# Moving sixteen blocks of transposes and a reused key/value group in a two-layer attention kernel: where the kept group is scored, and where its values are turned

## The chip, the cores and the metric

The kernel runs on one core of one Trainium2 chip. Times are device microseconds (us) of whole executions. The profile is one execution taken by the hardware profiler, so its span is one sample. All timed runs used here are undisturbed (fast).

## The reference

Two layers, each attention with cached keys and values followed by an MLP, run forward and then backward from `grad_out`. Both layers use the same caches and the same weights.

```python
x = A_x                                   # [2, 1, 1024]
x = x + attn(layernorm(x), k_cache, v_cache, wq, wo)   # layer 0
x = x + mlp(layernorm(x), w1, b1, w2, b2)              # the mlp has a layernorm of its own
x = x + attn(layernorm(x), k_cache, v_cache, wq, wo)   # layer 1
x = x + mlp(layernorm(x), w1, b1, w2, b2)
# outputs: x and the gradients of x, both caches, wq, wo, w1, b1, w2, b2
# caches: [2, 4, 16384, 128] bf16, 33.5 MB each; 32 query heads, 8 for each key/value head
```

Batch and key/value head together make `G` = 8 *groups*. A group's keys are four *chunks* of 1 MB, and so are its values. A layer's attention reads 67 MB of cache, and the caches are read by both layers, forward and backward.

## The kernel before

Loads go through a ring of seven 1 MB buffers (pool `ld`) and are all issued by one queue, in program order. A load is issued when the buffer of the seventh load before it is released. The last group (`G - 1` = 7) is *kept*: layer 0 loads its eight chunks into tiles of their own, and later uses load nothing. One more chunk, the first of group `XG` = 3, is kept in the same way (tiles `keepxK` and `keepxV`).

```python
    NLD = 7                                # load buffers of 1 MB
    ld = ctx.enter_context(tc.tile_pool(name="ld", bufs=NLD))
    # ...
    def turn(view, new_tp):                # transposes eight 128x128 blocks in place
        tp = new_tp()
        for o in range(8):
            PE.transpose(tp[:, o, :], view[:, o * 128:(o + 1) * 128], ident[:])
        evac_bf16(view, tp[:].rearrange("p a b -> p (a b)"), 1024)   # ScalarE or VectorE
    # ...
    def kv_load(w, g, c):
        keep = w + str(c) if g == G - 1 else w if (g, c) == (XG, 0) else None
        t = held_tiles[keep] if keep else ld.tile([128, LDW], BF16, name="kv_" + w, tag="ld")
        if keep not in held:
            src = Kv if w == "K" else Vv
            nc.sync.dma_start(t[:]..., src[g, :, c * TC:(c + 1) * TC, :])
            if keep:
                held.add(keep)
        return t[:].rearrange("p (t d) -> p t d", d=128)
```

The attention forward walks through slots, four to a chunk. A slot transposes 1024 keys (8 transposes) and scores those of two slots ago (8 matmuls). When a group's 16 slots are over, its softmax and its products with V follow, spread over the slots of the next group, beginning nine slots later.

```python
    def attn_fwd(l, q_bf, rbc, oT, groups):
        sch = Sched()
        slots = [(g, c, b) for g in groups for c in range(NCH) for b in range(NB)]
        # ... post(g): row maximum, 16 exponentials, sch.later(9, quads of chunks 0, 1),
        #     sch.later(13, quads of chunks 2, 3), evacuation, finish
            def finish(ps):
                V.tensor_tensor(out=oT[:, g, :], in0=ps, in1=rbc[:, g, :], op=ALU.mult)
        # ...
        while s < len(slots) + 2 or sch.busy():
            # ... emit_T(cv, b, True); sch.run_slot(...); score(s - 2)
    # ...
        attn_fwd(l, qT_bf, rbc, oT, ALLG)          # groups 0..7, the kept one last
```

The backward attention of layer 1 transposes V instead, and needs the kept group's V transposed. That is done there by the 16 *turns* (`v_turns`), one in every third slot. The kept group's own slots, which load and transpose nothing, lie between the slots of the third and the fourth group.

```python
    def attn_bwd(l, do_bf, dqT, dn, groups, ahead):     # groups 0, 4, 3, 1, 5, 2, 6
        slots = []
        for i, g in enumerate(groups):
            for c in range(NCH):
                for b in range(NB):
                    slots.append((g, c, b))
                    if 2 <= i < 2 + NCH // 2 and c % 2 == 0:
                        slots.append((G - 1, (i - 2) * 2 + c // 2, b))
        # ...
        v_turns = deque(lambda c=c, b=b: turn(held_tiles["V%d" % c][:, b * 1024:(b + 1) * 1024], ...)
                        for c in range(NCH) for b in range(NB))
        while s < len(slots) + 2 or sch.busy():
            # ...
                    kTs[s] = emit_T(cv, b, True)
                    if s % 3 == 2 and s >= 8 and v_turns:
                        v_turns.popleft()()
            # ...
            if dots and s % 3 < 2:          # dot products on VectorE with wq tiles of the ring
                dots.popleft()()
```

Of the kernel before, what the change touches and what calls it, by code (L numbers as in the profile page):

```python
# [9 lines left out]
BF16 = mybir.dt.bfloat16  # L10
# [13 lines left out]
def kernel(  # L24
# [25 lines left out]
    V = nc.vector  # L50
# [13 lines left out]
    G = B * HKV  # L64
    T = SK // 128
    TC = 32
    NCH = T // TC
# [254 lines left out]
    def turn(view, new_tp):  # L322
# [4 lines that stand above are left out]
        evac_bf16(view, tp[:].rearrange("p a b -> p (a b)"), 1024)  # L327
# [176 lines left out]

    def attn_fwd(l, q_bf, rbc, oT, groups):
        sch = Sched()
        slots = [(g, c, b) for g in groups for c in range(NCH) for b in range(NB)]
        kTs, sc, st = {}, {}, {}

        def max_half(g, f):  # L510
            m = small.tile([128, 8], F32, name="mx%d" % f)
            V.tensor_reduce(out=m[:], in_=sc[g][f][:], axis=AX.X, op=ALU.max)
            charge("D", 0.7)
            st[g].append(m)

        def post(g):
            max_half(g, 1)
            m0, m1 = st[g]
            V.tensor_tensor(out=m0[:], in0=m0[:], in1=m1[:], op=ALU.max)
            esum = small.tile([128, 2, 8], F32, name="esum")  # L520
            negm = small.tile([128, 8], F32, name="negm")
            box = {}

            def p1():
                box["pm"] = pm_([8, 128], F32, "pm")
                PE.transpose(box["pm"][:, :], m0[:], identf[:])
                gm = small.tile([8, 1], F32, name="gm")
                V.reduce_max(out=gm[:], in_=box["pm"][:, :], axis=AX.X)
                box["dg"] = small.tile([8, 8], F32, name="dg")
                V.tensor_scalar(out=box["dg"][:], in0=identf[0:8, 0:8], scalar1=gm[:, 0:1], scalar2=None, op0=ALU.mult)  # L530
                charge("D", 0.5)

            def p2():
                pm2 = pm_([128, 8], F32, "pm2")
                PE.matmul(pm2[:], lhsT=onesf[0:8, :], rhs=box["dg"][:], start=True, stop=True)
                V.tensor_scalar(out=negm[:], in0=pm2[:], scalar1=-1.0, scalar2=None, op0=ALU.mult)  # L536
                charge("D", 0.2)

            def ex(f, h):
                half = NP // 2  # L540
                S.activation(out=e_all[:, g, f * half:(f + 1) * half, l, h, :],  # L541
                             in_=sc[g][f][:, h, :].rearrange("p (a b) -> p a b", b=2),
                             func=ACT.Exp, bias=negm[:, h:h + 1], scale=1.0, accum_out=esum[:, f, h:h + 1])
                charge("A", 0.3)

            def fin1():
                V.tensor_tensor(out=esum[:, 0, :], in0=esum[:, 0, :], in1=esum[:, 1, :], op=ALU.add)

            def fin2():
                pm3 = part_sum(esum[:, 0, :], 8, "pm3")  # L550
                V.reciprocal(out=rbc[:, g, :], in_=pm3[:])

            def finish(ps):
                V.tensor_tensor(out=oT[:, g, :], in0=ps, in1=rbc[:, g, :], op=ALU.mult)

            a = Acc(g, "V", lambda u: e_all[:, g, u, l].rearrange("p h t -> p (h t)"), finish, g % 2)
            sch.later(2, p1)
            sch.later(4, p2)
            for i in range(16):
                sch.later(5 + i // 2, lambda i=i: ex(i // 8, i % 8))  # L560
            sch.later(9, lambda: queue_acc(sch, a, range(0, 2), False))
            sch.later(13, lambda: queue_acc(sch, a, range(2, 4), True))
            sch.later(14, fin1)
            sch.later(15, fin2)

        def score(s):
            g, c, b = slots[s]
            if c == 0 and b == 0:
                sc[g] = {}
                st[g] = []  # L570
            kT = kTs.pop(s)
            for j in range(8):
                t = c * TC + b * 8 + j
                f = t // TH
                if t % TH == 0:
                    sc[g][f] = px([128, 8, TH], F32, "sc")
                PE.matmul(sc[g][f][:, :, t % TH], lhsT=kT[:, j, :], rhs=q_bf[:, g, :], start=True, stop=True)  # L577
            if c == NCH // 2 - 1 and b == NB - 1:
                max_half(g, 0)
            if c == NCH - 1 and b == NB - 1:  # L580
                post(g)

        cv = None
        s = 0
        while s < len(slots) + 2 or sch.busy():
            sch.s = s
            if s < len(slots):
                g, c, b = slots[s]
                if b == 0:
                    cv = kv_load("K", g, c)  # L590
                kTs[s] = emit_T(cv, b, True)
            sch.run_slot(1 if s < len(slots) else 2)
            if 2 <= s < len(slots) + 2:
                score(s - 2)
            s += 1

    def attn_bwd(l, do_bf, dqT, dn, groups, ahead):
        sch = Sched()
        wq_q, wq_n, w2_q = deque(), {}, deque()
        slots = []  # L600
        for i, g in enumerate(groups):
            for c in range(NCH):
                for b in range(NB):
                    slots.append((g, c, b))
                    if 2 <= i < 2 + NCH // 2 and c % 2 == 0:
                        slots.append((G - 1, (i - 2) * 2 + c // 2, b))
        kTs, sc, accs = {}, {}, {}
        made = {"n": 0}
        done_g = []
# [60 lines left out]
        def score(s):  # L670
# [7 lines left out]
            if b == NB - 1:  # L678
# [1 line left out]

        cv = None
        s = 0
        v_turns = deque(lambda c=c, b=b: turn(held_tiles["V%d" % c][:, b * 1024:(b + 1) * 1024],
                                              lambda: pt([128, 8, 128], BF16, "turn"))
                        for c in range(NCH) for b in range(NB))
        while s < len(slots) + 2 or sch.busy():
            sch.s = s
            if s < len(slots):
                g, c, b = slots[s]
                if g == G - 1:  # L690
                    kTs[s] = kept_vT(c)[:, b * 8:(b + 1) * 8, :]
                else:
                    if b == 0:
                        cv = kv_load("V", g, c)
                    kTs[s] = emit_T(cv, b, True)
                    if s % 3 == 2 and s >= 8 and v_turns:
                        v_turns.popleft()()
                if g == groups[-1] and b == 1 and c == 0:
                    n = wq_n[g % HKV] = wq_steps(l, g % HKV, dqT, dn, lambda: pt([128, 8, 128], BF16, "wtq"),
                                                 lambda: px([128, 512], F32, "dn_ps"))  # L700
                    for k, f in enumerate(n[0]):
                        wq_q.append(lambda f=f, k=k, n=n: (f(), n[2][4 * k]()))
                        wq_q.extend(n[2][4 * k + 1:4 * k + 4])
            sch.run_slot(1 if s < len(slots) else 2)
            if 2 <= s < len(slots) + 2:
                score(s - 2)
            if wq_q and (s % 2 == 1 or len(wq_q) > 6):
                wq_q.popleft()()
            if dots and s % 3 < 2:
                dots.popleft()()  # L710
            s += 1
# [39 lines left out]
    def attn_layer_fwd(l, xT):  # L751
        y, rstd = ln_fwd(xT[:], f"a{l}")
        V.tensor_copy(out=n_all[:, :, lsl(l)], in_=y[:])
        qps, _ = w_pass(A_wq, D, HD, "q_ps", xT_bf=n_all[:, :, lsl(l)])
        qT_bf = vec.tile([128, G, 8], BF16, name=f"qT_bf{l}")
        for b in range(2):
            V.tensor_scalar(out=qT_bf[:, b * HKV:(b + 1) * HKV, :].rearrange("p k r -> p (k r)"), in0=qps[:, :, b],
                            scalar1=QSCALE, scalar2=None, op0=ALU.mult)
        rbc = vec.tile([128, G, 8], F32, name=f"rbc{l}")
        oT = vec.tile([128, G, 8], F32, name=f"oT{l}")  # L760
        attn_fwd(l, qT_bf, rbc, oT, ALLG)
        for b in range(2):
            V.tensor_copy(out=o_all[:, :, 2 * l + b], in_=oT[:, b * HKV:(b + 1) * HKV, :].rearrange("p k r -> p (k r)"))
        aps, _ = w_pass(A_wo, HD, D, "a_ps", xT_bf=o_all[:, :, lsl(l)])
        xn = vec.tile([128, DJ, 2], F32, name=f"xA{l}")
        V.tensor_tensor(out=xn[:], in0=aps[:], in1=xT[:], op=ALU.add)
        saved[f"a{l}"] = dict(y=y, rstd=rstd, qT_bf=qT_bf, rbc=rbc, oT=oT)
        return xn
# [695 lines left out]
```

## Time and profile before

| | |
|---|---|
| median of 3 runs | 1150.4 us (1148.43 to 1152.41) |
| bytes moved | 449.3 MB, mean 391 GB/s |
| highest rate that a stretch holds | about 424 GB/s |

The first lines are of the page of the kernel before. The GB/s line has 40 slices of 28.8 us each.

```profile
span 1150.5 us, 39958 instructions
...
GB/s 371 423 425 424 425 424 412 407 353 357 423 424 424 423 318 423 394 355 406 376 420 421 340 366 357 318 281 304 374 405 423 419 421 421 424 422 420 424 422 248
```

At 424 GB/s the 449.3 MB take 1060 us, so the transfers bound the kernel and the rest is hollows in this line. The unit of this document is the *lost time* of a stretch: its length times (1 - GB/s / 424). The sum of lost time is what a schedule can win or lose, since both kernels move the same bytes.

The next fence is the windows view of the kernel before. Each row gives a stretch (us), its length, the busy time of TensorE (PE), its weight loads, VectorE, ScalarE and GpSimd with the number of instructions, then the granted TensorE clock, the busy share of the DMA engines, and GB/s. The rows are the first 50 us after the layer-1 query projection (the *head*), the end of that attention forward with the output projection (the *tail*), and the first 60 us, the middle and the last 50 us of the backward attention.

```profile
272.50:322.50 50.00, 44.86 (x951) 40.00 (x952) 26.18 (x55) 24.23 (x90) 0.00 (x0) 0.94 1.01 424
400.00:440.00 40.00, 28.50 (x592) 22.25 (x590) 12.80 (x44) 10.94 (x67) 1.38 (x2) 0.69 0.89 346
502.50:562.50 60.00, 57.34 (x1258) 48.27 (x1259) 32.94 (x73) 26.96 (x47) 0.00 (x0) 1.00 0.95 367
562.50:617.50 55.00, 48.26 (x958) 39.56 (x956) 31.98 (x76) 27.10 (x49) 0.00 (x0) 0.91 1.01 422
617.50:667.50 50.00, 37.99 (x749) 31.21 (x747) 22.37 (x64) 21.58 (x39) 0.00 (x0) 0.86 0.97 372
```

Lost time: head 0, tail 40 x (1 - 346/424) = 7.4 us, backward 8.1 us in the first 60 us, 0.3 in the middle and 6.1 at the end. In the first 60 us TensorE is busy 57 of 60.

The tile view of the kernel before says where the turns are and what one costs (minimum/median/maximum ns, then first and last start):

```profile
L326 PE MATMUL turn<-ident,keepV x128: 217/219/219, 509.5 to 563.3; 128*128 128x128 bf16 x128
L161 DVE COPY keepV<-turn x8: 690/691/692, 510.1 to 544.4; 128x1024 bf16<-128x1024 bf16 x8
L158 ACT COPY keepV<-turn x8: 586/587/593, 513.5 to 563.6; 128x512 int32<-128x512 int32 x8
```

The load queue at the head, from its timeline (start, time taken, line, what is loaded). Seven K tiles are issued as the query weights leave the ring. Then each release brings the next load: in these lines every 2.6 to 3.2 us, from 4 us after the projection on, and the transfers never run dry:

```profile
265.15 7.48 SPq L413 DMA_DIRECT2D kv_K<-in_A_k_cache_dram  x7
276.83 0.33 SPq L413 DMA_DIRECT2D kv_V<-in_A_v_cache_dram  x1
280.05 0.33 SPq L413 DMA_DIRECT2D kv_K<-in_A_k_cache_dram  x1
282.63 0.33 SPq L413 DMA_DIRECT2D kv_V<-in_A_v_cache_dram  x1
285.22 0.33 SPq L413 DMA_DIRECT2D kv_K<-in_A_k_cache_dram  x1
```

Three pieces of the same stretch, TensorE's timeline of the kernel before: a slot of transposes and scores repeats every 0.65 us.

```profile
281.35 0.61 PE L424 MATMUL tp<-ident,kv_K 128*128 128x128 bf16 x8
281.80 0.35 PE L577 MATMUL sc<-qT_bf,kT 128*128 128x8 bf16 x8
282.00 0.61 PE L424 MATMUL tp<-ident,kv_K 128*128 128x128 bf16 x8
```

### The profile page before, as it was taken

How to read it: one execution, taken by the hardware profiler on the slowest of the kernel's cores; microseconds unless marked ns; L12 is line 12 of the kernel's file. 1: busy time of each engine (PE TensorE's matmuls, PEld its weight loads, DVE VectorE, ACT ScalarE, POOL GpSimd, SP SyncE). 2: the span in 40 equal slices, each digit the busy share in tenths (PEclk: the TensorE clock that was granted, in tenths of full speed). 3: DMA queues.
4: the chain of work that ended last, by engine and by line, in shares of the span. 5: the costliest groups of instructions: out<-in, count | busy, mean ns of one | idle time of the engine just before them, and what ended most of it. 6: DMA issues, size and time to landing. Idle time of an engine off the chain costs nothing. (4 is left out here: it accounts for less than half of the span.)

```text
span 1150.5 us, 39958 instructions
## 1 busy us (share of the span) xinstructions
PE 956.2 (83%) x17581; PEld 732.7 (64%) x17581; DVE 632.4 (55%) x1335; ACT 567.0 (49%) x1417; POOL 63.9 (6%) x113
## 2 busy tenths in 40 slices
PE   4989795487879876899987799788898999998885
PEld 3867674487767755888776698665555554554452
DVE  1535451133545433454845365667777867787684
ACT  0544351022535430344454455567676867786673
POOL 0000000000000000000000000001111112111111
PEclk9988895587999975899997899797777967898785
DMA  9999999998999989999999999877999999999996
GB/s 371 423 425 424 425 424 412 407 353 357 423 424 424 423 318 423 394 355 406 376 420 421 340 366 357 318 281 304 374 405 423 419 421 421 424 422 420 424 422 248
DMA packets 89130, 449.30 MB, mean 391 GB/s; under 512 B 7026, under 2 KB 7026, under 8 KB 49788
## 3 DMA queue, kind: packets, MB, share of 16 engines
q1 hardware_dynamic: 72204, 348.17, 75.0%
q0 software_dynamic: 16752, 98.59, 20.7%
q8 instruction: 137, 2.24, 0.7%
q14 instruction: 37, 0.30, 0.1%
HBM read 348.14 MB, written 98.58 MB: 388 GB/s over the span
## 5 line engine op out<-in xcount | busy, mean ns | idle before, releaser
L158 ACT COPY kT<-tp 128x512 int32<-128x512 int32 x209 | 122.8, 587 | 252.5 <-PE tp L424 243.6
L161 DVE COPY kT<-tp 128x1024 bf16<-128x1024 bf16 x159 | 108.6, 690 | 110.8 <-PE tp L424 97.6
L424 PE MATMUL tp<-ident,kv_K 128*128 128x128 bf16 x1728 | 144.6, 233 | 4.3 <-DMA kv_K<-in_A_k_cache_dram 4.3
L424 PEld LDWEIGHTS <-kv_K 128*128 128x128 bf16 x1728 | 109.7, 104 | 5.0 <-DMA kv_K<-in_A_k_cache_dram 4.9
L169 DVE CAST big<-xm 128x512 bf16<-128x512 f32 x142 | 92.3, 685 | 31.8 <-PE xm L1242 13.9
L166 ACT CAST big<-xm 128x512 bf16<-128x512 f32 x155 | 84.4, 593 | 25.9 <-PE xm L1144 15.5
L577 PEld LDWEIGHTS <-kT 128*128 128x128 bf16 x2048 | 76.3, 98 | 27.0 <-issue 22.0
L577 PE MATMUL sc<-qT_bf,kT 128*128 128x8 bf16 x2048 | 91.8, 171 | 0.0
L274 PE MATMUL wtp<-ident,wt 128*128 128x128 bf16 x928 | 77.8, 233 | 3.7 <-issue 2.3
L424 PE MATMUL tp<-ident,kv_V 128*128 128x128 bf16 x864 | 70.9, 229 | 10.3 <-DMA kv_V<-in_A_v_cache_dram 8.8
L541 ACT ACTIVATE e_all<-sc,negm 128x64 bf16<-128x64 f32 x256 | 77.1, 343 | 1.1 <-DVE negm L536 1.0
L310 PEld LDWEIGHTS <-wt 128*128 128x128 bf16 x1696 | 48.8, 103 | 43.6 <-issue 14.7
L169 DVE CAST keepK<-xm 128x512 bf16<-128x512 f32 x95 | 61.6, 684 | 16.2 <-PE xm L1242 9.6
L456 PE MATMUL acc_all<-kv_V,e_all 128*16 128x256 bf16 x864 | 46.2, 294 | 27.9 <-DMA kv_V<-in_A_v_cache_dram 13.8
L161 DVE COPY wT<-wtp 128x1024 bf16<-128x1024 bf16 (+1 forms) x64 | 40.5, 636 | 49.0 <-PE wtp L274 45.9
L158 ACT COPY wT<-wtp 128x512 int32<-128x512 int32 (+1 forms) x60 | 34.5, 576 | 65.5 <-PE wtp L274 56.8
L166 ACT CAST keepK<-xm 128x512 bf16<-128x512 f32 x102 | 54.8, 592 | 24.1 <-PE xm L1242 21.3
L166 ACT CAST keepV<-xm 128x512 bf16<-128x512 f32 (+1 forms) x98 | 53.1, 594 | 22.5 <-PE xm L1242 18.9
L424 PEld LDWEIGHTS <-kv_V 128*128 128x128 bf16 x864 | 55.9, 102 | 11.9 <-DMA kv_V<-in_A_v_cache_dram 9.5
L274 PEld LDWEIGHTS <-wt 128*128 128x128 bf16 x928 | 59.6, 104 | 4.4 <-issue 3.1
L541 ACT ACTIVATION_READ_ACCUMULATOR e_all<-sc,negm 128x1 f32 x256 | 59.8, 234 | 0.0
L169 DVE CAST keepV<-xm 128x512 bf16<-128x512 f32 (+1 forms) x74 | 48.0, 684 | 15.3 <-PE xm L1242 12.7
(352 smaller groups left out, 1775.8 us busy)
## 6 DMA issues: line engine op xcount, KB each, us to landing
kv_K<-in_A_k_cache_dram SPq DMA_DIRECT2D x81, 1024.0 KB, 12.2
kv_V<-in_A_v_cache_dram SPq DMA_DIRECT2D x81, 1024.0 KB, 12.1
out_dram<-big POOLq DMA_DIRECT2D x36, 1024.0 KB, 17.4
wt<-in_A_wo_dram SPq DMA_DIRECT2D x32, 1024.0 KB, 10.0
wt<-in_B_w_dram SPq DMA_DIRECT2D x32, 896.0 KB, 14.0
out_dram<-keepK POOLq DMA_DIRECT2D x22, 1024.0 KB, 17.3
out_dram<-keepV POOLq DMA_DIRECT2D x18, 1024.0 KB, 17.1
wt<-in_A_wq_dram SPq DMA_DIRECT2D x16, 1024.0 KB, 8.8
```

The lines of the kernel that those rows point to most:

```text
L158: S.copy(out=dst.bitcast(I32), in_=src.bitcast(I32))
L161: V.tensor_copy(out=dst, in_=src)
L166: S.copy(out=dst, in_=src)
L169: V.tensor_copy(out=dst, in_=src)
L274: PE.transpose(tp[:, o, :], wv[:, j, (o0 + o) * 128:(o0 + o + 1) * 128], ident[:])
L310: PE.matmul(fps[:, jo, :].rearrange("p (a b) -> p a b", b=2), lhsT=wv[:, j, jo * 128:(jo + 1) * 128], rhs=xT_bf[:, j0 + j, :].unsqueeze(1) ...
L424: PE.transpose(tp[:, j, :], cv[:, b * 8 + j, :], ident[:])
L456: PE.matmul(self.acc[cg:cg + 16, :], lhsT=coef(u), rhs=self.cv[:, t:t + 2, :].rearrange("p t d -> p (t d)"), start=False, stop=True, tile_ ...
L541: S.activation(out=e_all[:, g, f * half:(f + 1) * half, l, h, :], in_=sc[g][f][:, h, :].rearrange("p (a b) -> p a b", b=2), func=ACT.Exp, ...
L577: PE.matmul(sc[g][f][:, :, t % TH], lhsT=kT[:, j, :], rhs=q_bf[:, g, :], start=True, stop=True)
```

## The change

The intent: in backward the turns compete for TensorE where it is full. If layer-1 forward begins with the kept group, that group's V is free early, and the turns can run in the rest of forward, where TensorE waits for transfers. The kept chunks of the backward stage are spread over three groups (one, two, one) instead of two (two, two).

```diff
     def attn_fwd(l, q_bf, rbc, oT, groups):
+        v_turns = deque()
 ...
             def finish(ps):
                 V.tensor_tensor(out=oT[:, g, :], in0=ps, in1=rbc[:, g, :], op=ALU.mult)
+                if g == groups[0] == G - 1:
+                    v_turns.extend((c, b) for c in range(NCH) for b in range(NB))
 ...
             sch.run_slot(1 if s < len(slots) else 2)
+            if v_turns and s % 3 == 0:
+                vc, vb = v_turns.popleft()
+                turn(held_tiles["V%d" % vc][:, vb * 1024:(vb + 1) * 1024], lambda: pt(...))
 ...
     def attn_bwd(l, do_bf, dqT, dn, groups, ahead):
+        kept_at = [(1, 2), (2, 0), (2, 2), (3, 0)]
 ...
-                    if 2 <= i < 2 + NCH // 2 and c % 2 == 0:
-                        slots.append((G - 1, (i - 2) * 2 + c // 2, b))
+                    if (i, c) in kept_at:
+                        slots.append((G - 1, kept_at.index((i, c)), b))
 ...
-        v_turns = deque(lambda c=c, b=b: turn(...) for c in range(NCH) for b in range(NB))
 ...
-                    if s % 3 == 2 and s >= 8 and v_turns:
-                        v_turns.popleft()()
 ...
-        attn_fwd(l, qT_bf, rbc, oT, ALLG)
+        attn_fwd(l, qT_bf, rbc, oT, ALLG if l == 0 else ALLG[-1:] + ALLG[:-1])
```

More of the change, by code (lines that the diff above doesn't have):

```diff
@@ L592, in attn_fwd @@
             sch.run_slot(1 if s < len(slots) else 2)
+            if v_turns and s % 3 == 0:
+                vc, vb = v_turns.popleft()
+                turn(held_tiles["V%d" % vc][:, vb * 1024:(vb + 1) * 1024], lambda: pt([128, 8, 128], BF16, "turn"))
             if 2 <= s < len(slots) + 2:
@@ L682, in attn_bwd @@
         s = 0
-        v_turns = deque(lambda c=c, b=b: turn(held_tiles["V%d" % c][:, b * 1024:(b + 1) * 1024],
-                                              lambda: pt([128, 8, 128], BF16, "turn"))
-                        for c in range(NCH) for b in range(NB))
         while s < len(slots) + 2 or sch.busy():
```

## The prediction

> **What bounds it now.** The profile's header counts 449.3 MB at a mean of 391 GB/s; the 40-slice row tops out at about 424 GB/s. At 424 the bytes alone take 1060 us (my estimate) of the 1150 us, so the transfers bound the kernel and about 90 us is lost in hollows of that row. The page "DMA: Bandwidth & Descriptors" of the Trainium skill (section "Where 436 GB/s comes from") puts the ceiling at 435 GB/s; this trace never holds more than some 425.
>
> The hollows that the change touches (windows view, my cuts):
> - End of layer-1 attention forward, 415-430 us: DMA share 0.66, 237 GB/s: 6.6 us lost. The kept group, last, loads nothing; the seven load buffers already hold output weights.
> - Backward attention of layer 1: 500-515 us at 316 GB/s (3.8 us lost), 515-550 at 408 (1.3 us), 550-560 at 288 (3.2 us). TensorE is 98% busy from 515 to 560.
> Layer-1 forward at 270-400 us has no hollow.
>
> **What moves.** The 16 V turns (8 transposes each; median copy 690 ns on VectorE, 586 ns on ScalarE, tile view) go from backward to forward. A turn adds about 0.45-0.5 us to TensorE's stream (timeline), so 7-8 us of TensorE work leaves the backward stage. In forward a slot without PV product takes 0.645 us (timeline, 280-287 us), a product adds 0.4 us: 16 x 0.645 + 8 x 0.4 = 13.5 us of TensorE per group, against 8 x 2.47 = 19.8 us of loads. The turns add about 2.5 us per group: they hide.
>
> **What is given back.** With the kept group first, seven K tiles load (issued 265-272, done by about 284 us), and then the ring is full until the first non-kept slots release a tile (about 286 us, plus start-up latency). Then tiles come free every 2.6 us, later every 3.4 us, until V tiles flow too at about 304 us. I count 6-7 us of idle DMA between 284 and 304 us. That about cancels the 6.6 us won at the end, whose tail should now look like layer 0's (408 GB/s).
>
> **Backward.** Without turns, and with one kept chunk in the second group, two in the third, one in the fourth, TensorE needs about 14 us plus 2.2 us per kept chunk, below 19.8. So I expect most of the loss of 510-560 us back, but not that of 500-510 (do/delta chain) and not all of 550-560, part of which is load buffers held by wq tiles until VectorE's dot products are done (the load queue's waits: 14.5 us on that accumulation). Gain 3-5 us. Later stages are transfer-bound, so it carries through.
>
> **Prediction.** Forward +0.5 (-3 to +4), backward -4 (-6 to -1): 1147 us, range 1140 to 1154. Faster by over 2%: 4%; within 2%: 94%; slower by over 2%: 2%.
>
> **What would show each step.** (1) A new hollow of 5-8 us of lost transfer time at the start of layer-1 attention (about 284-304 us). (2) The hollow before the output weights at 415-430 gone. (3) Turn copies of keepV at about 305-350 us with DMA still at 424 there. (4) Backward, first 60 us: DMA at 405 GB/s or more except the first 10 us.
>
> **What would make it wrong.** A smaller or larger start-up hollow; the half-rate clock: the skill's "TensorE: Matmul & The Clock Gate" (Part 1, "What's actually happening") says idleness throttles and activity releases; the trace agrees (0.50 in 340-350 us, between waits). Or the backward hollows are buffer waits and stay.

## The result

| | before | after |
|---|---|---|
| median | 1150.89 us (4 runs, 1148.43 to 1152.41) | 1155.68 us (4 runs, 1154.95 to 1157.16) |
| ratio | | 1.0045, 95% interval 1.0024 to 1.0067 |

The changed kernel is about 5 us slower. That is within 2%, which the prediction gave 94%; but it expected the time to fall by 3 to 4 us, and it rose. A ratio here is the mean time of one kernel's fast runs over that of the other's of the same rounds, so it is not quite the ratio of the medians. The effect is small, but the interval leaves out 1. The measured time lies above the predicted range (1140 to 1154).

The page of the changed kernel, the same two lines. Slices 10 and 11 of the row (259 to 317 us) show 331 and 290 GB/s where before had 357 and 423; slice 15 has 412 where before had 318.

```profile
span 1153.0 us, 39955 instructions
...
GB/s 371 424 425 424 424 424 412 405 364 331 290 418 413 423 412 423 396 360 418 407 420 414 302 365 368 311 290 292 395 419 423 422 420 420 424 423 420 424 422 248
```

The windows view of the changed kernel, for the same five stretches (its query projection ends 1 us earlier, its backward attention starts 5 us later):

```profile
271.50:321.50 50.00, 46.62 (x1015) 41.28 (x1014) 27.62 (x57) 26.14 (x93) 0.00 (x0) 0.98 0.86 322
400.00:440.00 40.00, 22.32 (x464) 16.81 (x457) 7.03 (x24) 5.69 (x37) 0.00 (x0) 0.58 1.03 415
507.50:567.50 60.00, 55.95 (x1253) 45.49 (x1253) 32.90 (x77) 22.74 (x39) 0.00 (x0) 1.00 0.98 391
567.50:622.50 55.00, 44.97 (x877) 36.92 (x874) 35.57 (x82) 27.04 (x50) 0.00 (x0) 0.91 1.02 421
622.50:672.50 50.00, 36.39 (x693) 30.04 (x686) 15.34 (x50) 19.33 (x35) 0.00 (x0) 0.83 0.90 341
```

Lost time: head 50 x (1 - 322/424) = 12.0 us (before 0), tail 0.8 (7.4), backward first 60 us 4.7 (8.1), middle 0.4 (0.3), end 9.8 (6.1). So the tail was repaired and the turns' share of the backward loss came back, as intended. But the head opened by 12 us, and the end of the backward stage lost 3.7 us more.

The load queue at the head of the changed kernel. After the seven K tiles nothing is issued until 285.55, because no tile of the ring is used before the kept group's 16 slots are over. After that, up to 309.48, the releases come 3.2 to 5.0 us apart, while a load takes 2.5 us (1 MB at 424 GB/s):

```profile
263.90 7.71 SPq L413 DMA_DIRECT2D kv_K<-in_A_k_cache_dram  x7
285.55 0.33 SPq L413 DMA_DIRECT2D kv_V<-in_A_v_cache_dram  x1
288.71 0.33 SPq L413 DMA_DIRECT2D kv_K<-in_A_k_cache_dram  x1
292.31 0.33 SPq L413 DMA_DIRECT2D kv_V<-in_A_v_cache_dram  x1
295.76 0.33 SPq L413 DMA_DIRECT2D kv_K<-in_A_k_cache_dram  x1
300.74 0.33 SPq L413 DMA_DIRECT2D kv_V<-in_A_v_cache_dram  x1
304.72 0.33 SPq L413 DMA_DIRECT2D kv_K<-in_A_k_cache_dram  x1
309.48 0.33 SPq L413 DMA_DIRECT2D kv_V<-in_A_v_cache_dram  x1
310.47 0.33 SPq L413 DMA_DIRECT2D kv_K<-in_A_k_cache_dram  x1
```

TensorE sets that pace. Its timeline in the changed kernel has products with the kept V between the slots (they load nothing), and now and then a wait. Transposes to transposes, these three slots take 1.99, 0.76 and 1.08 us. The second has no product, but a small matmul of the softmax (`pm`):

```profile
298.11 0.61 PE L424 MATMUL tp<-ident,kv_K 128*128 128x128 bf16 x8
299.56 0.40 PE L456 MATMUL acc_all<-keepV,e_all 128*16 128x256 bf16 x8 [0.84 <-DVE acc_all L439]
299.89 0.36 PE L580 MATMUL sc<-qT_bf,kT 128*128 128x8 bf16 x8
300.10 0.61 PE L424 MATMUL tp<-ident,kv_K 128*128 128x128 bf16 x8
300.55 0.27 PE L527 MATMUL pm<-identf,mx 128*8 128x128 f32 x1
300.65 0.35 PE L580 MATMUL sc<-qT_bf,kT 128*128 128x8 bf16 x8
300.86 0.61 PE L424 MATMUL tp<-ident,kv_K 128*128 128x128 bf16 x8
301.39 0.40 PE L456 MATMUL acc_all<-keepV,e_all 128*16 128x256 bf16 x8
301.72 0.36 PE L580 MATMUL sc<-qT_bf,kT 128*128 128x8 bf16 x8
301.94 0.61 PE L424 MATMUL tp<-ident,kv_K 128*128 128x128 bf16 x8
```

From 285.6 to 310.5 us the trace has 200 key transposes (25 slots), 80 product matmuls (10 quads) and one turn in 24.9 us, so 1.0 us a slot. A slot with nothing but transposes and scores still takes 0.65 us there, one with a product 1.08. The rest is in a few slots: three in which TensorE waits (1.67, 1.99 and 2.82 us, with waits of 0.52, 0.84 and 0.69), and four with softmax matmuls (0.1 to 0.4 us more each).

The turns are where they were meant to be (tile view of the changed kernel):

```profile
L326 PE MATMUL turn<-ident,keepV x128: 219/219/230, 308.2 to 361.5; 128*128 128x128 bf16 x128
```

### The profile page after: what moved, and what is told of

Its sections match the earlier page's. It is cut to its first block, busy times and chain, and to the rows that moved or that the text cites. A ratio compares the mean times of both kernels' runs of the same rounds, so it can differ in the third digit from the quotient of the medians.

```text
span 1153.0 us, 39955 instructions
## 1 busy us (share of the span) xinstructions
PE 947.0 (82%) x17581; PEld 723.6 (63%) x17581; DVE 634.3 (55%) x1337; ACT 565.4 (49%) x1415; POOL 63.7 (6%) x113
## 3 DMA queue, kind: packets, MB, share of 16 engines
q0 software_dynamic: 16752, 98.59, 20.6%
## 5 line engine op out<-in xcount | busy, mean ns | idle before, releaser
L424 PE MATMUL tp<-ident,kv_K 128*128 128x128 bf16 x1728 | 136.3, 224 | 3.2 <-DMA kv_K<-in_A_k_cache_dram 2.5
L424 PEld LDWEIGHTS <-kv_K 128*128 128x128 bf16 x1728 | 103.2, 100 | 4.0 <-DMA kv_K<-in_A_k_cache_dram 3.0
L274 PE MATMUL wtp<-ident,wt 128*128 128x128 bf16 x928 | 75.3, 228 | 4.0 <-issue 2.6
L169 DVE CAST keepV<-xm 128x512 bf16<-128x512 f32 (+1 forms) x74 | 48.1, 685 | 15.8 <-PE xm L1244 12.5
## 6 DMA issues: line engine op xcount, KB each, us to landing
wt<-in_B_w_dram SPq DMA_DIRECT2D x32, 896.0 KB, 14.4
```

What stands on the lines that cost most here:

```text
L169: V.tensor_copy(out=dst, in_=src)
L274: PE.transpose(tp[:, o, :], wv[:, j, (o0 + o) * 128:(o0 + o + 1) * 128], ident[:])
L424: PE.transpose(tp[:, j, :], cv[:, b * 8 + j, :], ident[:])
```

## The experiments

The theories at the start. **A:** the loss in forward is the order; a group without loads stops a full ring. **B** (rival): the loss in forward is the turns, which fill TensorE. For backward, **C:** the new places of the kept chunks cost something. **D:** the end of the stage is held by ring buffers that wait for dot products.

Tables give lost time as defined above, from each run's own trace. *Head* is the 50 us after the layer-1 query projection. *To backward* is from that projection to the scaled output gradient. *First 60* and *end* (after 115 us) are parts of the backward stage.

### The order alone

```diff
 # kernel before, and only:
-        attn_fwd(l, qT_bf, rbc, oT, ALLG)
+        attn_fwd(l, qT_bf, rbc, oT, ALLG if l == 0 else ALLG[-1:] + ALLG[:-1])
```

> Only the order of the groups in layer-1 forward is changed: kept group first, turns still in the backward stage, kept chunks two and two. Theory A (the loss is the order: no loads for the kept group's 16 slots, so the ring of seven buffers stands full at the start): the 12 us of lost transfer time at the start of the forward stage is nearly all here already (8 to 12 us), the 6 us at its end is gone, backward as in before; 3 to 6 us slower than before. Rival B (the loss is the turns, which fill TensorE in the forward stage): start hollow 5 us or less, time equal to before within 2 us.

Measured: 1156.34 us against 1150.73, ratio 1.0047 (1.0022 to 1.0071). The windows row of its head:

```profile
271.00:321.00 50.00, 45.51 (x991) 40.19 (x990) 27.04 (x57) 24.66 (x90) 0.00 (x0) 0.97 0.86 327
```

That is 11.5 us lost, with no turn in forward. Backward lost 15.3 us, much as before. The order makes the head's hollow, and the turns add at most about a microsecond to it (12.0 and 12.7 in two profiles of the changed kernel). B is refuted.

### Order and turns, old places

```diff
 # changed kernel, and only:
-        kept_at = [(1, 2), (2, 0), (2, 2), (3, 0)]
+        kept_at = [(2, 0), (2, 2), (3, 0), (3, 2)]
```

> The changed kernel with the kept chunks of the backward stage back at two and two; kept group first, turns in forward. Theory A: same forward stage as the changed kernel. Backward: if the new spread is what lost the 4 us again at the end of the stage (rival C), the stage from the scaled output gradient to the first w2 backward product is 160 to 162 us instead of 165.1, and the run is 3 to 4 us faster than the changed kernel (about 1152); if the end of the stage is held by the load ring and the dot products whatever the spread (theory D), the stage is 164 to 166 us and the time is the changed kernel's, 1155.

Measured: 1153.58 us, ratio 1.0024 (1.0000 to 1.0047). Backward lost 13.4 us and its stage took 163.3 us, between the two forecasts. Against the order alone, the time is 2.8 us lower: that is what moving the turns is worth here (the means differ by 2.6 us, with about 2.5 on either side). The turns' copies leave VectorE and ScalarE with them (33 and 27 us busy of the first 60, against 57 for TensorE); no run separates the two. The new places put about 2 us back on top in the changed kernel, with overlapping intervals.

### The places alone

```diff
 # kernel before, and only the kept_at list of the changed kernel
+        kept_at = [(1, 2), (2, 0), (2, 2), (3, 0)]
-                    if 2 <= i < 2 + NCH // 2 and c % 2 == 0:
-                        slots.append((G - 1, (i - 2) * 2 + c // 2, b))
+                    if (i, c) in kept_at:
+                        slots.append((G - 1, kept_at.index((i, c)), b))
```

> Only the new places of the kept chunks in the backward stage; forward order and turns as before. Forward must equal before (no start hollow). Theory D (end of the stage held by ring and dots): stage 164 to 166 us, time within 1.5 us of before. Rival C (the new places cost something): stage 167 to 169 us, 3 to 4 us slower than before.

Measured: 1155.41 us, ratio 1.0044 (1.0010 to 1.0077). Forward equals before (head 0 lost). Backward took 168.5 us, which is C's forecast:

```profile
502.50:562.50 60.00, 57.14 (x1251) 48.24 (x1252) 31.15 (x70) 25.70 (x45) 0.00 (x0) 1.00 0.91 349
```

The first 60 us lost 10.6 us, where before lost 8.1. I had counted the new places as a gain; they cost.

### The kept group third

```diff
 # changed kernel, and:
-        ... ALLG if l == 0 else ALLG[-1:] + ALLG[:-1]
+        ... ALLG if l == 0 else ALLG[:2] + ALLG[-1:] + ALLG[2:-1]
-                if g == groups[0] == G - 1:
+                if g == G - 1 and l == 1:
-            a = Acc(..., finish, g % 2)
+            a = Acc(..., finish, groups.index(g) % 2)
```

> The changed kernel with the kept group third in layer-1 forward instead of first (and the accumulator half chosen by place in the order, so that neighbours do not share one); turns follow its finish as in the changed kernel. Theory A: in mid-stream the ring is not full, so the kept slots let the transfers catch up rather than stop: the start hollow of 12 us shrinks to 0 to 3 us and the end hollow stays away, so forward plus the stage up to the backward attention is 9 to 12 us shorter than in the changed kernel and the whole run takes 1143 to 1147. Rival B (turns cost): the turns are still in forward, so the run stays within 3 us of the changed kernel's 1155.7.

Measured: 1150.76 us, ratio 0.9997 (0.9973 to 1.0020), so it equals the kernel before. But the reason given was wrong: the hollow did not shrink to 3 us, it moved. The windows row and the load queue of this run, 50 to 80 us after the projection:

```profile
320.50:350.50 30.00, 28.36 (x610) 23.58 (x607) 17.16 (x38) 17.42 (x78) 0.00 (x0) 1.00 0.82 308
```

```profile
325.86 0.33 SPq L413 DMA_DIRECT2D kv_K<-in_A_k_cache_dram  x1
329.31 0.33 SPq L413 DMA_DIRECT2D kv_V<-in_A_v_cache_dram  x1
338.69 0.33 SPq L413 DMA_DIRECT2D kv_K<-in_A_k_cache_dram  x1
```

30 x (1 - 308/424) = 8.2 us lost. The queue stands for 9.4 us between two issues, because the buffer that is next in turn holds the second K chunk of group 3, loaded early (issued at 313.05), and its four slots run only from 334.8 to 338.7 us. Until then TensorE has work that frees no buffer: products with the kept V, and from 329.8 to 334.8 us the slots of group 3's first chunk, which is kept too. The queue waits for that one tile. So the hollow comes after the kept group's slots (296 to 313 us), and the other kept chunk has a share in it that no run separates. A hollow stood at all three places tried: 12 us when the group is first, about 8 when third, about 7 when last.

### Third, with the old places

> Kept group third in forward, turns in forward, kept chunks of backward two and two as before. If the places of the kept chunks matter (2.9 us between the changed kernel and its run with the old places), this is 1 to 3 us faster than the run with the kept group third and the new places (1150.8): 1148 to 1150. If the places do not matter, 1150 to 1152.

Edit: the run before with `kept_at = [(2, 0), (2, 2), (3, 0), (3, 2)]`. It was run at another time. Measured: 1152.57 us, ratio 1.0011 (0.9991 to 1.0031). The first 60 us lost 3.8 instead of 4.8 us, but the time did not fall; in this pair the places do not show in the time.

### The turns between the layer norms

After layer-1 attention, TensorE has little to do while two layer norms run on VectorE, and the kept group's V is no longer needed as it was. So the order and the places stay as in the kernel before, and the 16 turns go there, all copied by ScalarE.

```diff
 # kernel before, v_turns and its use removed from attn_bwd, and:
-    def ln_fwd(xT, name):
+    def ln_fwd(xT, name, turns=(0, 0)):
         ps = part_sum(s1[:], 2, "ln_ps")
+        turn_kept(turns[0])                      # emits so many turns
 ...
         ps2 = part_sum(s2[:], 2, "ln_ps2")
+        turn_kept(turns[1])
 ...
     def mlp_hidden(l, xT):
-        y1, rstd1 = ln_fwd(xT[:], f"m{l}a")
-        y2, rstd2 = ln_fwd(y1[:], f"m{l}b")
+        if l == 1:
+            v_turns.extend((c, b) for c in range(NCH) for b in range(NB))
+        copies_on("A" if l == 1 else None)
+        turn_kept(1)
+        y1, rstd1 = ln_fwd(xT[:], f"m{l}a", (2, 5))
+        y2, rstd2 = ln_fwd(y1[:], f"m{l}b", (2, 6))
+        copies_on(None)
```

> Order and places of the chunks as before; the 16 turns are neither in the attention forward nor in the attention backward, but between the layer norms of the second MLP, where TensorE has almost nothing to do and the transfers run at 420 GB/s anyway. Theory A: no start hollow, forward up to attention backward within 1.5 us of before (lost time 10 to 11 us), backward without turns loses 11 to 13.5 us instead of 14.4: 1147 to 1150, faster than both kernels. If moving the turns out of backward is worth nothing because the end of that stage takes the gain back, it equals before: 1150 to 1152.

Measured: 1146.60 us against 1151.15, ratio 0.9957 (0.9937 to 0.9978). It beats both kernels. The repeat, on another chip:

> The variant with the turns between the layer norms once more, on the same chip as its partner with the new places: again 3 to 6 us faster than before (0.995 to 0.997); lost time in the first 60 us of backward 3.5 again.

Measured: 1147.03 us, ratio 0.9966 (0.9948 to 0.9985). The tile view and two windows rows (head; first 60 us of backward) of the first of the two runs:

```profile
L328 PE MATMUL turn<-ident,keepV x128: 216/219/315, 429.1 to 442.3; 128*128 128x128 bf16 x128
```

```profile
271.50:321.50 50.00, 44.66 (x951) 39.55 (x952) 25.91 (x53) 24.59 (x90) 0.00 (x0) 0.96 1.01 424
500.00:560.00 60.00, 56.74 (x1241) 47.11 (x1241) 35.22 (x82) 24.95 (x44) 0.00 (x0) 0.97 0.98 400
```

The turns are done in 13 us, but not in the shadow of the norms: from the end of the attention's output projection to the first matmul of the MLP it is 13.0 us (12.4 in the repeat), where the kernel before needs 8.0. The longer wait costs little, because the transfers run on (415 GB/s from 429 to 442.3 us) and the MLP's matmuls then find more of their weights loaded (196 in a row without a wait, against 140 before). The head has no hollow, and the first 60 us of backward lose 3.5 us instead of 8.1. Backward as a whole lost 9.8 and 10.7 us in the two profiles, against 14.4 and 14.1 before: the 4 us that I had forecast for that stage do exist.

### Dot products in every slot

```diff
 # changed kernel, and only:
-            if dots and s % 3 < 2:
+            if dots:
```

> The changed kernel, but the dot products of the backward stage (each holds a wq tile in the load ring until it is done) are issued in every slot instead of two slots of three. Theory D (the end of the stage is held by ring buffers that wait for dot products): the lost time of the last 45 us of the stage falls from about 10 us to 6 or less and the run is 3 to 5 us faster than the changed kernel (1151 to 1153). If dots do not hold the ring: no change (1155 to 1157), or slower because VectorE's copies come later in the first half.

Measured: 1157.88 us, ratio 1.0057 (1.0038 to 1.0076). The end lost 5.1 us instead of 7 to 10, as D had it, but the middle of the stage lost 3.5 instead of 0.4 and nothing was gained. Where the dot products stand decides where the hollow falls, not how much is lost. As an explanation of the time, D falls.

### How much is chance

> The changed kernel once more, for a second profile: how much of a stage's lost transfer time is chance. If the profiles are repeatable, lost time from the first query projection of layer 1 to the attention-backward start is 17 us again and in the backward stage 14 to 15.5 us; if the end of the backward stage is chance, the latter may fall anywhere from 11 to 15 (11 was seen in the run with the kept group third, whose backward program is nearly the same).

> The kernel before, for a second profile, to size what is chance. Lost time from the first query projection of layer 1 to the attention backward 10 us again, in the backward stage 13.5 to 15.5, of it 8 in the first 60 us and 6 after 115 us; the last stage, in which the first profile lost 2 to 3 us more than any other run, 38 to 40.

Edits: none. Single runs, for their traces.

| profile | head | to backward | first 60 | end | backward in all | after the stage |
|---|---|---|---|---|---|---|
| before | 0 | 10.3 | 8.1 | 6.0 | 14.4 | 51.2 |
| before, again | 0 | 10.7 | 8.0 | 5.7 | 14.1 | 47.1 |
| changed | 12.0 | 17.0 | 4.7 | 9.8 | 14.8 | 48.0 |
| changed, again | 12.7 | 17.0 | 5.0 | 7.0 | 12.5 | 49.5 |

In these four profiles head, way to backward and first 60 us repeat within 0.7 us. For the head and the first 60 us two later pairs agree (turns between the norms, without and with the new places), but there the way to backward moved too: 9.7 and 11.0 us, 11.7 and 14.2. The end of the backward stage moved by 2.8 us between two profiles of one program, and what follows the stage by up to 4 us. So the changed kernel's extra loss at that end (9.8 and 7.0 against 6.0 and 5.7) is partly chance, and its cause stays open.

### Six load buffers

```diff
-    NLD = 7
+    NLD = 6
```

> The changed kernel with six load buffers instead of seven, to test that the start hollow is a full ring: one buffer less holds one load (2.5 us of transfers) less when the kept group begins. Theory A: the lost time in the first 50 us after the query projection rises from 12.0 to 14 to 16 us, elsewhere losses rise too. If the hollow has another cause (latency of the loads, order on the queue), it stays within 1 us of 12.

> The kernel before with six load buffers: start of the forward stage still without a hollow (under 1 us in the first 50 us), the hollow at its end, where the ring fills with output weights, grows from 7 to 9 to 10 us.

Measured (single runs): changed 1174.66 us, before 1179.49 us. The head of the changed kernel and the tail of the kernel before:

```profile
275.00:325.00 50.00, 47.20 (x1022) 41.84 (x1022) 27.51 (x56) 26.80 (x97) 0.00 (x0) 0.97 0.83 308
405.00:445.00 40.00, 28.22 (x606) 22.39 (x603) 11.48 (x36) 11.61 (x68) 0.69 (x1) 0.72 0.84 311
```

The changed kernel's head lost 50 x (1 - 308/424) = 13.7 us, just under the range. Against 12.0 and 12.7 with seven buffers that is too little to settle anything. The kernel before lost nothing at the head and 40 x (1 - 311/424) = 10.7 us at its tail instead of 7.4. For the tail that fits a full ring, though it is one profile and lies just above the forecast of 9 to 10. At the head one buffer less cost less than the 2.5 us of one load; with the pace shown above this suggests that the pace of the releases, not only the depth of the ring, makes that hollow.

### Both: turns between the norms and the new places

> The faster variant (turns between the layer norms, kept group last) with the new places of the kept chunks as well. If the places matter only while the turns share the backward stage (the spread alone cost 4.7 us with them there), this is within 1.5 us of the variant without them: 1145 to 1148.5. If the new places cost in themselves, 1149 to 1151.

> Its partner with the new places. Theory E: lost time in the first 60 us of backward 5 to 6 us against 3.5, so 1.5 to 4 us slower than the variant without the new places. If the 5.7 us of the first comparison were chance of the chip, within 1 us of it.

Edit: the variant with the turns between the norms, with the `kept_at` list of the changed kernel. Measured: 1152.32 us, ratio 1.0010 (0.9984 to 1.0036), and again 1153.17 us, ratio 1.0020 (1.0006 to 1.0035). With the old places it was 0.9957 and 0.9966. My first expectation, that the places only matter while turns share the stage, is refuted: without them the new places cost 5.7 us (two chips) and 6.1 us (one chip). The first 60 us explain some of it (lost 6.0 and 5.9 against 3.5 and 3.1). The pairs also differ by 2 and 3 us of lost time before the backward stage begins, where the two programs have the same instructions on TensorE. Two profiles of one program differ there by 1.3 and 2.5 us, so that part may be chance; it is not explained, and so the full 6 us are not either.

### Later places

```diff
 # kernel before with kept_at, but:
+        kept_at = [(2, 2), (3, 0), (3, 1), (3, 2)]
```

> The kernel before with one kept chunk of the backward stage moved the other way, out of the third group into the fourth (its last chunk stays where it was). Theory E (loadless TensorE work in the first 60 us): lost transfer time there falls from 8.0 to 6 to 7 us, time 1 to 3 us below before. If spreading as such or the order of chunks is what costs, the time does not fall: 0 to 3 us above before, since the chunks now lie closer together.

Measured: 1152.48 us, ratio 1.0008 (0.9991 to 1.0026). The first 60 us lost 7.0 instead of 8.0, as theory E has it; the middle lost 1.5 instead of 0.3, and the time did not fall. All runs with seven buffers, between 20 and 60 us of the backward stage:

| run | kept slots scored | turns | lost, us |
|---|---|---|---|
| turns between norms (2 profiles) | 12, 12 | 0 | 0.3, 0.3 |
| order and turns, old places; third, old places | 12, 12 | 0 | 0.4, 0.2 |
| changed (2); third; dots in every slot | 16, 16, 16, 16 | 0 | 1.3, 1.5, 1.2, 2.1 |
| between norms, new places (2) | 15, 15 | 0 | 2.6, 0.8 |
| later places | 7 | 10 | 2.7 |
| before (2); order alone | 10, 10, 10 | 11 | 4.2, 3.5, 4.3 |
| places alone | 12 | 12 | 6.3 |

Work that needs no load, put into a stretch where TensorE is already full, costs transfer time. Both the turns and the early kept chunks are such work. The two profiles of one program at 2.6 and 0.8 show how far a single figure can be trusted. This holds for the stretch; it was not shown that every microsecond of it reaches the end of the kernel.

## Why the prediction was wrong

1. **"I count 6-7 us of idle DMA between 284 and 304 us. That about cancels the 6.6 us won at the end."** This is the step that failed in forward: the mechanism was right and the term was mis-sized. Measured: 12.0 and 12.7 us, from about 283 to 320 us. The won end was right (7.4 to 0.8 us). The pace was the error. I added 0.645 us a slot and 0.4 us a product, which for the 25 slots, 10 products and one turn of 285.6 to 310.5 us gives 20.6 us. The trace has 24.9 us. The slot itself was right (0.65 us) and the product nearly (0.43). What the sum left out is in seven slots: about 2.8 us in three in which TensorE waited for the zeroed accumulator or for exponentials (2.05 us of waits, and the matmuls that reduce an accumulator), and about 1.1 us of softmax matmuls in four others. These 4.3 us are most of the 5 to 6 us by which the hollow was put too small (an estimate: the same loads, spread over 24.9 instead of 20.6 us). I had also measured 2.6 us for the first releases and let them run too long. Forward thus cost about 6.5 us (lost time to backward 17.0 and 17.0 against 10.3 and 10.7) where the sum said 0.5.
2. **"So I expect most of the loss of 510-560 us back ... Gain 3-5 us."** The removal of the turns did that: 3.0 to 3.4 us came back in the first 60 us, and from 10 us on the transfers ran at 409 GB/s there (380 before), as sign (4) asked. But the stage as a whole lost 14.8 and 12.5 us, against 14.4 and 14.1. The step that failed is counting the new places of the kept chunks as harmless because TensorE's 14 us plus 2.2 us a chunk stay below 19.8 us. Averages over a group hide that the first 60 us have no slack and the next 55 do: the new places move kept work from the slack into the full stretch. The places alone cost 4.7 us, and about 6 us on top of the fastest variant; with the kept group third they cost nothing (1150.76 us with the new places, 1152.57 with the old), so the size, and why it reaches the time, stays open. A further 1 to 4 us at the end of the stage is partly chance and not explained.
3. **"The turns add about 2.5 us per group: they hide."** Right. The head lost 11.5 us without them and 12.0 to 12.7 with them, and from 320 to 360 us the transfers hold 408 to 429 GB/s in all but one 5 us step.
4. **The clock.** The page "TensorE: Matmul & The Clock Gate" of the Trainium skill (Part 1, "What's actually happening") says that the default state is throttled and activity releases it. The trace agrees (0.98 in the changed kernel's busy head, 0.58 in its tail, which waits for weights), and so the hollow did not slow what came after it: TensorE was the busy engine in it. The 0.50 at 340 to 350 us that the prediction names follows three waits of TensorE in the kernel before (0.67, 1.65 and 1.21 us, the last ending at 341.2); from then to 350 us it works without one.
5. **The sum, in times:** the order costs 5.6 us, moving the turns wins 2.8, the new places cost 2.1, which makes 4.9 us; the result is 4.8. By construction these nearly add up; the intervals of the steps are about 2.5 us wide on each side.

## What to carry to other kernels

In this transfer-bound kernel with a ring of buffers in order, a whole group of compute that loads nothing led to a full ring and a waiting queue at each of the three places tried. What it costs depends on the pace at which buffers are *released* afterwards, which is to be read from the trace with its bubbles and not added up from durations. The section "Optimization Strategy" of the page "Perfetto Trace Analysis" of the Trainium skill says that interleaving regimes with different limits may help; here the one variant that beat the kernel before (by 0.3 to 0.4%) put the work between the layer norms, where it made TensorE's part 5 us longer but left the transfers running. When three edits come in one change, run each alone: here the one with the sound reason was worth 2.8 us and the two beside it cost more.

## What the Trainium skill lacked or had wrong

- "Perfetto Trace Analysis", "What 'DMA-bound' means", lists the DMA engines, the issuing sequencer and SBUF reads. No entry covers a load queue that stands still because the next buffer in order is not released: 12 us in the head of the changed kernel, and 9.4 us between two issues in the run with the kept group third. The nearest sentence, on consistent bubbles under "Optimization Strategy", speaks of missing buffers; with one buffer fewer the tail's hollow grew from 7.4 to 10.7 us, the head's only from about 12.4 to 13.7.
- "DMA: Bandwidth & Descriptors", "Where 436 GB/s comes from", says that for transfers between HBM and SBUF the HBM side (about 358 GB/s) binds. With one core at work these runs hold 424 GB/s over 50 us and longer; the same passage also gives a measured 425 GB/s, which agrees. "Perfetto Trace Analysis", "Roofline", has the single-core case right (about 435 GB/s as the ceiling).
- No page says how repeatable one profile is: between two profiles of one program, the head and the first 60 us of backward repeated within 0.7 us, the way to backward moved by up to 2.5 us, the end of the backward stage by up to 2.8, and what follows it by up to 4.
